# Seven products instead of eight in four more pairs of output blocks, with their sums gathered in one PSUM bank

## The chip, the cores and the metric

The kernel runs on one core of a Trainium2 chip. The metric is the device time of one execution in microseconds (us). In the text PE is TensorE (matmuls), ACT is ScalarE, DVE is VectorE, POOL is GpSimd and SP is SyncE, which here only issues transfers.

## The reference

Attention with a sliding window of 128 positions and a linear distance bias (8 batches of 8 heads, 576 positions, 64 channels) feeds a two-layer block with an ELU between the layers. All its 4608 rows go through both weight matrices:

```python
scores = scale * np.matmul(q, k.transpose(0, 1, 3, 2))        # 8 x 8 x 576 x 576
scores = np.where(mask, scores + bias[None], -1000000000.0)   # mask: 0 <= i - j < 128
attn = softmax(scores)
x = np.matmul(attn, v)  ->  (4608, 512)
h = x @ w_in                                                  # w_in 512 x 2048
g = np.where(h > 0.0, h, np.exp(np.minimum(h, 0.0)) - 1.0)
out = g @ w_out                                               # w_out 2048 x 512
```

## The kernel before, in words

The rows are taken in 9 tiles of 512. For each tile the *hidden* layer is made in 16 steps; in the later tiles a step is 256 rows by 2 chunks of 128 hidden channels: 8 matmuls of 256 columns (16 of 128 columns in earlier tiles) into one of two PSUM banks hp. ACT then takes an exponential into e, either by one step of ACT and a clamp on POOL (lines 310 and 311), or, where the step's slot is in the set SOFT, by two steps of ACT (307 and 308) and none of POOL. DVE combines e and the bank into g (`elu`, line 318), which also frees the bank for the hidden step after next.

Everything is laid out by hand in numbered *slots*. A slot holds one hidden step, the `elu` of the slot before, whatever stands in `tasks` for that slot (loads, transposes `turn_qk`, `weigh`, `all_values`, sums), a share of output in `OUT`, and what stands in `late` (combinations, attention `scores`). Each engine gets its instructions in the order in which the slots' lists are walked through, so what is queued ahead of what is decided here. Slot 24 has the hidden matmuls that start at 55.91 us of the profile, slot 42 those at 91.41, slot 88 those at 184.59, slot 134 those at 275.39 and slot 149, the last, those at 300.43.

The attention of a batch is four units of 128 keys. A unit puts its scores at the end of a slot; the next two slots each have two exponentials of ACT in front (`expo`, line 231) and one `weigh` on DVE (line 236); the slot after that has the product with v on PE (`all_values`), normalised by DVE and transposed into xT by a transfer from SP. This goes on until slot 133.

The *output* layer is made per pair n of two blocks of 128 rows (18 pairs). An ordinary pair takes 32 matmuls of 512 columns, 4 in each of 8 slots (`output`, line 324), a copy of each block by ACT (`store`, line 331) and a transfer from SP. The pairs in the list SEVEN, 11 of the 18, are computed as a 2 x 2 block product by seven multiplications (Winograd's form): g and w_out are cut in quarters, DVE makes four sums of g's quarters (`sums`, tiles S1 to S4, line 348, on 128 x 1024 elements in fp16), and once for all pairs four differences of w_out's quarters (`quarters`, tiles T1 to T4, in halves, in slots 25 to 32). Then seven products of 8 matmuls with 256 columns each follow (`product`, line 392), 7 matmuls in each of the pair's 8 slots, which begin at slot s = 15 + 8n. They are issued in the order of `turns`: 1, 6, 2, 7, 5, 4, 3.

The four output quarters are sums of the products: C11 = M1 + M2, U2 = M1 + M6, U3 = U2 + M7, C12 = U2 + M5 + M3, C22 = U3 + M5, C21 = U3 plus M4. Before the change ACT copies M1 out of PSUM into U1 and the finished C11 into the output tile ob, and DVE makes six additions per pair with one operand in PSUM (`combine`). Two banks (op and av, which change places after every such pair) each hold two halves:

```python
        turns = [(i, j) for i in (1, 6, 2, 7, 5, 4, 3) for j in range(8)]
        ...
        def places(n):
            x, y = XY[n]
            return ((x, 0), (y, 0), (x, 256), (y, 256)) if n < 2 * NTB - 1 else (
                (sp[2], 0), (sp[3], 0), (sp[0], 0), (hp[0], 0), (av, 0))
```

The last pair, 17, has no hidden steps beside it but the first ones, and is written out separately at the end of the slots (slots 148 to 152), with its last product split into two halves of 128 columns.

Of the kernel before, what the change touches and what calls it, by code (L numbers as in the profile page):

```python
# [18 lines left out]
def kernel(  # L19
# [9 lines left out]
    nc = tc.nc  # L29
    B, H, S, D = q.shape  # L30
    NTOK, DO = out.shape
    FF = moe_w_in.shape[1]
    NFC = FF // 128
    NTB = NTOK // 512
# [3 lines left out]
    V = nc.vector  # L38
# [35 lines left out]
    sp = [spa[:, 0, :], spa[:, 1, :]] + [ps_s.tile([128, 512], F32, name=f"sp{i}", tag=f"sp{i}") for i in (2, 3)]  # L74
    hp = [ps_h.tile([128, 512], F32, name=f"hp{i}", tag=f"hp{i}") for i in range(2)]
    av = ps_v.tile([128, 512], F32, name="av", tag="av")
# [72 lines left out]
    with tc.manual_schedule():  # L149
# [142 lines left out]
        def hidden(t, c0, w, f0, nf, p, soft):  # L292
            hps[t, c0, f0] = p
            a = (512 * t + c0) % RING
            cuts = [(0, w, a)] if a + w <= RING else [(0, RING - a, a), (RING - a, w, 0)]
            for l in range(nf):
                fc = f0 + l
                for u0, u1, x0 in cuts:
                    for c in range(4):
                        nc.tensor.matmul(  # L300
                            p[:, l * w + u0:l * w + u1], w_in_sb[:, c, fc * 128:(fc + 1) * 128],
                            xT[:, c, x0:x0 + u1 - u0], start=(c == 0), stop=(c == 3))
            e = es[t, c0, f0] = work.tile([128, 512], F32, name="e", tag="e", bufs=6)
            n = w * nf
            if soft:

                nc.scalar.activation(e[:, 0:n], p[:, 0:n], AF.Relu, scale=-1.0)  # L307
                nc.scalar.activation(e[:, 0:n], e[:, 0:n], AF.Exp, scale=-1.0)  # L308
                return
            nc.scalar.activation(e[:, 0:n], p[:, 0:n], AF.Exp)  # L310
            nc.gpsimd.tensor_scalar(out=e[:, 0:n], in0=e[:, 0:n], scalar1=1.0, scalar2=0.0,  # L311
                                    op0=ALU.min, op1=ALU.max)
# [25 lines left out]

        WB = lambda i, k: w_out_sb[:, 8 * i:8 * i + 8, 256 * k:256 * k + 256]

        def A(n, i, k):
            c = 256 * (n % 2) + 128 * i
            return gs[n // 2][:, 8 * k:8 * k + 8, c:c + 128]

        def add(o, a, b, op=ALU.add):
            V.tensor_tensor(out=o, in0=a, in1=b, op=op)  # L348

        def quarters(i, half):  # L350
            h = slice(4 * half, 4 * half + 4)
            a, b = {1: (WB(0, 1), WB(0, 0)), 2: (WB(1, 1), T[1]), 3: (WB(1, 1), WB(0, 1)), 4: (WB(1, 0), T[2])}[i]
            add(T[i][:, h, :], a[:, h, :], b[:, h, :], ALU.subtract)
# [8 lines left out]
                    3: lambda: (A(n, 0, 0), A(n, 1, 0)), 4: lambda: (A(n, 0, 1), SS[n, 2])}[i]()  # L362
            add(SS[n, i][:, j, :], a[:, j, :], b[:, j, :], ALU.add if i == 1 else ALU.subtract)

        def places(n):


            x, y = XY[n]
            return ((x, 0), (y, 0), (x, 256), (y, 256)) if n < 2 * NTB - 1 else (
                (sp[2], 0), (sp[3], 0), (sp[0], 0), (hp[0], 0), (av, 0))  # L370

        def place(n, i):
            o, c = places(n)[(0, 0, 4 if n == 2 * NTB - 1 else 2, 3, 2, 1, 1)[i - 1]]
            return o[:, c:c + 256]

        def kept(n, i):
            if (n, i) not in U:
                U[n, i] = work.tile([128, 256], F32, name=f"U{i}", tag=f"U{i}", bufs=1)
            return U[n, i]

        def tile_out(n, i):
            if (n, i) not in obs:
                obs[n, i] = work.tile([128, DO], F32, name="ob", tag="ob")
            return obs[n, i]

        def product(n, i, j0=0, j1=8, o=None, c0=0, c1=256):
            a, b = {1: lambda: (A(n, 0, 0), WB(0, 0)), 2: lambda: (A(n, 0, 1), WB(1, 0)), 3: lambda: (SS[n, 4], WB(1, 1)),
                    4: lambda: (A(n, 1, 1), T[4]), 5: lambda: (SS[n, 1], T[1]), 6: lambda: (SS[n, 2], T[2]),
                    7: lambda: (SS[n, 3], T[3])}[i]()
            o = place(n, i) if o is None else o  # L390
            for j in range(j0, j1):
                nc.tensor.matmul(o[:, 0:c1 - c0], a[:, j, :], b[:, j, c0:c1], start=j == 0 and (i in (1, 4, 5, 6) or o is av and n == 2 * NTB - 1),  # L392
                                 stop=j == 7, skip_group_check=True)
            if j1 == 8 and i == 1:
                nc.scalar.copy(kept(n, i), o)
            if j1 == 8 and i == 2:
                nc.scalar.copy(tile_out(n, 0)[:, 0:256], o)

        def combine(n, what):
            if what == "U2":  # L400
                add(kept(n, 2), kept(n, 1), place(n, 6))
            elif what == "U5":
                add(kept(n, 2), kept(n, 2), place(n, 5))
            elif what == "U3":
                add(kept(n, 3), kept(n, 1), place(n, 7))
            elif what == "C22":
                add(tile_out(n, 1)[:, 256:512], kept(n, 3), place(n, 5))
                if n == 2 * NTB - 1:
                    put(n, 1, 256, DO)
            elif what == "C12":  # L410
                add(tile_out(n, 0)[:, 256:512], kept(n, 2), place(n, 3))
                put(n, 0, 0, DO)
            else:
                add(tile_out(n, 1)[:, 0:256], kept(n, 3), place(n, 4))
                put(n, 1, 0, DO)

        def put(n, i, c0, c1):
            r = 256 * n + 128 * i
            nc.sync.dma_start(out[r:r + 128, c0:c1], tile_out(n, i)[:, c0:c1])

        def last_piece(n, o, c0, c1):
            product(n, 4, 0, 8, o, c0, c1)
            add(tile_out(n, 1)[:, c0:c1], kept(n, 3)[:, c0:c1], o[:, 0:c1 - c0])
            put(n, 1, c0, c1)

        wz = one([128, 256], F16, "wz")

# [69 lines left out]
        early, tasks, late, HID, OUT = {}, {}, {}, {}, {}  # L497

        def at(s, f, *a):
            tasks.setdefault(s, []).append((f, a))  # L500

        def after(s, f, *a):
            late.setdefault(s, []).append((f, a))

# [13 lines left out]
        for t in range(2, NTB):  # L518
            for j in range(16):
                step = (128 * (j // 4), 128, 4 * (j % 4), 4) if t < 4 else (256 * (j // 8), 256, 2 * (j % 8), 2)  # L520
                HID[16 * t + 6 + j] = [(t, *step, BUF[(j + 1) % 2])]
        SEVEN = (17, 3, 5, 7, 9, 11, 12, 13, 14, 15, 16)

        XY = {1: (op, av)}
        for n in range(2, 2 * NTB):
            XY[n] = XY[n - 1][::-1] if n - 1 in SEVEN else XY[n - 1]
        for o in range(16 * NTB):
            t, ts, f = o // 16, o // 4 % 4, o % 4
            if o // 8 in SEVEN:
                continue  # L530
            s = (9, 11, 13, 14)[o] if o < 4 else 11 + o if o < 13 else 2 * o - 1 if o < 16 else 15 + o
# [70 lines left out]
        for b in range(2, B):  # L602
            for u in range(4):
                a = START[b] + 4 * u
# [11 lines left out]
            a = START[b - 1] if b > 2 else 0  # L616
            for n in range(4):
                piece = (b, int(n < 2), n % 2)
                if b == 2:
                    m = 4 if n < 2 else 6  # L620
# [7 lines left out]
                at(a + 3 + n if a else 20 + n // 2, load_v, b, n)  # L628


        for m in range(8):
            at(25 + m, quarters, 1 + m // 2, m % 2)
        turns = [(i, j) for i in (1, 6, 2, 7, 5, 4, 3) for j in range(8)]
        for n in SEVEN:
            s = 15 + 8 * n
            if n < 2 * NTB - 1:
                m = 6 if n >= 8 else 4
                for d, i, j in ((-2, 1, (0, m)), (-1, 1, (m, 8)), (0, 2, ()), (1, 3, ()), (3, 4, ())):
                    at(s + d, sums, n, i, *j)
                for d, what in ((2, "U2"), (4, "U3"), (5, "C22"), (6, "C21"), (7, "C12")):  # L640
                    after(s + d, combine, n, what)
                for d in range(8):
                    OUT[s + d] = [(product, (n, i, j, j + 1)) for i, j in turns[7 * d:7 * d + 7]]
            else:
                at(s - 3, sums, n, 3)
                for i in (1, 2):
                    at(s - 2, sums, n, i, 0, 6)
                    at(s - 1, sums, n, i, 6, 8)
                at(s - 1, product, n, 1)
                at(s, sums, n, 4)  # L650
                OUT[s] = [(product, (n, 2)), (product, (n, 6)), (combine, (n, "U2")), (product, (n, 5)), (combine, (n, "U5"))]
                OUT[s + 1] = [(product, (n, 3)), (combine, (n, "C12")), (product, (n, 7)), (combine, (n, "U3"))]
                OUT[s + 2] = [(combine, (n, "C22")), (last_piece, (n, hp[0], 128, 256)), (last_piece, (n, hp[1], 0, 128))]


        SOFT = {s for n in SEVEN for s in range(13 + 8 * n, 19 + 8 * n)} | set(range(25, 33)) | set(range(16 * NTB - 10, 16 * NTB + 8))

        slots = set(HID) | set(OUT) | set(tasks) | set(early)
        for s in range(min(slots), max(slots) + 1):
            for f, a in early.get(s, []):  # L660
                f(*a)
            for step in HID.get(s, []):
                hidden(*step, s in SOFT)
            if s - 1 in HID and s not in (1, 4, 5):
# [37 lines left out]
```

## Time and profile before

| | us |
|---|---|
| median of 13 runs | 314.57 (314.21 to 316.31) |
| the profiled execution itself | 314.57 |
| its span, first to last instruction | 312.8 |
| PE busy | 304.8 |
| DVE busy | 247.4 |
| ACT busy | 215.8 |
| POOL busy | 124.1 |
| elu, DVE, 128x512 | 0.683 each, 144 of them |
| sums and quarters, DVE, 128x1024 fp16 | 0.66 to 0.68 each |
| additions, DVE, 128x256 with an operand in PSUM | 0.41 each |
| copies, ACT, 128x256 from PSUM | 0.353 each |
| copies, ACT, 128x512 from PSUM (store) | 0.58 each |

The difference of 1.8 us between the execution's time and its span lies around the first and the last instruction. The granted clock of PE is 1.0 throughout. Busy times of PE come from modelled ends and overlap, so that the distance between the starts of consecutive groups tells more than a single duration: a matmul of 256 columns has a duration of 273 ns but the next one starts about 110 ns later. On DVE and ACT too, the next instruction starts some 0.08 to 0.1 us before the row of the last one ends.

### The profile page before, as it was taken

The page shows a single profiled execution, that of the slowest core. Times are in us where ns is not written, and L with a number is a line of the kernel's source. Part 1 is how long each engine was busy: PE and PEld are TensorE (multiplying, and loading weights), DVE is VectorE, ACT ScalarE, POOL GpSimd, SP SyncE. Part 2 cuts the span into 40 slices and gives each one's busy share as a digit, 9 for nine tenths or more (in the row PEclk, how much of TensorE's full clock was granted, in tenths as well). Part 3 has the DMA queues.
Part 4 walks back from the last instruction along what each step waited for, and adds up shares of the span by engine and source line. Part 5 has one row for each costly group of instructions (what it writes and reads, how often), then busy time and mean ns, then how long its engine had stood idle before and what let it go on. Part 6 is the DMA issues. An engine that isn't in the chain of part 4 may idle for free.

```text
span 312.8 us, 10024 instructions
## 1 busy us (share of the span) xinstructions
PE 304.8 (97%) x4191; PEld 245.1 (78%) x4191; DVE 247.4 (79%) x489; ACT 215.8 (69%) x392; POOL 124.1 (40%) x190
## 2 busy tenths in 40 slices
PE   8899999999999999999999999999999999999995
PEld 6788874876788778987787678767889888888884
DVE  4747556898789878886897698778999889887883
ACT  4666458798686368656875588549787878768760
POOL 8947879611804562464336542663201010100000
PEclk9999999999999999999999999999999999999999
DMA  9999999990995939295929991999140202030102
GB/s 96 199 195 207 199 174 140 172 140 10 102 116 78 145 58 146 26 171 84 128 34 165 118 122 23 125 156 135 11 103 20 78 17 86 19 94 0 70 35 103
DMA packets 96510, 32.05 MB, mean 102 GB/s; under 512 B 83920, under 2 KB 91984, under 8 KB 96464
## 3 DMA queue, kind: packets, MB, share of 16 engines
q0 software_dynamic: 75920, 18.36, 64.3%
q1 hardware_dynamic: 20544, 13.05, 16.5%
q8 instruction: 33, 0.54, 0.8%
q14 instruction: 13, 0.11, 0.2%
HBM read 36.70 MB, written 9.44 MB: 148 GB/s over the span
## 4 chain that ended last, share of the span: by engine, by line
PE 79%; DVE 9%; DMA 4%; ACT 3%; issue 3%; POOL 1%; DVEq 0%; ACTq 0%; POOLq 0%
PE hp L300 34%; PE av L392 9%; PE op L392 8%; PE op L324 7%; PE av L324 5%; PE spa L225 4%; PE spa L266 3%; DVE g L318 2%; DMA st<-in_q_dram 2%; DMA VP<-in_v_dram 2%; PE op L430 2%; ACT EX L231 1%; DVE xn L255 1%; PE sp L300 1%; PE sp L392 1%
## 5 line engine op out<-in xcount | busy, mean ns | idle before, releaser
L300 PE MATMUL hp<-xT,wi 128*128 128x128 f16 (+2 forms) x1744 | 144.9, 233 | 2.0 <-DVE g L318 1.7
L300 PEld LDWEIGHTS <-wi 128*128 128x128 f16 x1856 | 124.5, 98 | 24.2 <-issue 7.5
L318 DVE SCALAR_TENSOR_TENSOR g<-e,hp 128x512 f16<-128x512 f32 x138 | 94.3, 683 | 25.1 <-POOL e L311 18.4
L311 POOL TENSOR_SCALAR e<-e 128x512 f32<-128x512 f32 x71 | 44.5, 627 | 146.7 <-ACT e L310 146.2
L310 ACT ACTIVATE e<-hp 128x512 f32<-128x512 f32 x65 | 38.9, 599 | 39.6 <-PE hp L300 36.3
L307 ACT ACTIVATE e<-hp 128x512 f32<-128x512 f32 x73 | 43.6, 598 | 21.2 <-PE hp L300 17.3
L308 ACT ACTIVATE e<-e 128x512 f32<-128x512 f32 x73 | 46.1, 631 | 2.3
L236 DVE TENSOR_TENSOR EX<-EX,TAB 128x1024 f16<-128x1024 f16 x48 | 33.2, 691 | 14.4 <-ACT EX L231 14.1
L392 PEld LDWEIGHTS <-S 128*128 128x128 f16 x352 | 32.9, 98 | 5.0 <-DVE S L348 1.4
L114 POOL DMA_DIRECT2D VP<-in_v_dram x40 | 34.4, 872 | 0.7 <-DVE xn L255 0.7
L324 PE MATMUL op<-wo,g 128*128 128x512 f16 x128 | 32.9, 379 | 0.0
L231 ACT ACTIVATE EX<-spa 128x512 f16<-128x512 f32 x48 | 26.0, 595 | 8.6 <-PE spa L225 7.5
L324 PEld LDWEIGHTS <-g 128*128 128x128 f16 x224 | 19.3, 97 | 14.8 <-issue 1.1
L392 PEld LDWEIGHTS <-g 128*128 128x128 f16 x272 | 25.2, 98 | 2.6
L231 ACT ACTIVATE EX<-sp 128x512 f16<-128x512 f32 x48 | 25.9, 595 | 0.0
L324 PE MATMUL av<-wo,g 128*128 128x512 f16 x80 | 20.5, 379 | 0.0
L392 PE MATMUL av<-s,S 128*128 128x256 f16 x120 | 18.0, 273 | 0.2 <-DVE S L348 0.2
L392 PE MATMUL op<-s,S 128*128 128x256 f16 x120 | 18.0, 273 | 0.1
L272 DVE TENSOR_TENSOR xn<-spa,rden 128x512 f16<-128x512 f32 x24 | 16.6, 692 | 0.8
L348 DVE TENSOR_TENSOR S<-g 128x1024 f16<-128x1024 f16 (+3 forms) x33 | 16.6, 502 | 0.2
L108 POOL DMA_DIRECT2D st<-in_k_dram x24 | 16.4, 686 | 0.4 <-issue 0.3
L108 POOL DMA_DIRECT2D st<-in_q_dram x24 | 16.2, 677 | 0.1
(142 smaller groups left out, 373.3 us busy)
## 6 DMA issues: line engine op xcount, KB each, us to landing
out_dram<-ob SPq DMA_DIRECT2D x35, 256.0 KB, 2.9
VP<-in_v_dram POOLq DMA_DIRECT2D x32, 128.0 KB, 5.0
st<-in_k_dram POOLq DMA_DIRECT2D x24, 144.0 KB, 4.2
st<-in_q_dram POOLq DMA_DIRECT2D x24, 144.0 KB, 4.6
wi<-in_moe_w_in_dram POOLq DMA_DIRECT2D x4, 512.0 KB, 11.0
wo<-in_moe_w_out_dram POOLq DMA_DIRECT2D x4, 512.0 KB, 10.3
VP<-in_v_dram POOLq DMA_DIRECT2D x8, 64.0 KB, 5.0
s<-in_k_dram POOLq DMA_DIRECT2D x1, 512.0 KB, 12.2
```

The costliest lines, as they stand in the source:

```text
L108: nc.gpsimd.dma_start(st[b][32 * g:32 * g + 32, w, :, :, :, :].rearrange("p h n j d -> p (h n) (j d)"), (q, k)[w][b, 2 * g:2 * g + 2, :, : ...
L114: nc.gpsimd.dma_start(VP[b % 2][0:p, n, :, 0:D], v[b, :, 128 * n:128 * n + p, :].rearrange("h p d -> p h d"))
L231: nc.scalar.activation(unit(b, u)[:, g, :, :], sp[g].rearrange("p (h c) -> p h c", h=2), AF.Exp, scale=0.125)
L236: V.tensor_tensor(out=e, in0=e, in1=TAB[:, int(u == 3), 2 * gp:2 * gp + 2, :, :], op=ALU.mult)
L300: nc.tensor.matmul(p[:, l * w + u0:l * w + u1], w_in_sb[:, c, fc * 128:(fc + 1) * 128], xT[:, c, x0:x0 + u1 - u0], start=(c == 0), stop=(c ...
L307: nc.scalar.activation(e[:, 0:n], p[:, 0:n], AF.Relu, scale=-1.0)
L308: nc.scalar.activation(e[:, 0:n], e[:, 0:n], AF.Exp, scale=-1.0)
L310: nc.scalar.activation(e[:, 0:n], p[:, 0:n], AF.Exp)
L311: nc.gpsimd.tensor_scalar(out=e[:, 0:n], in0=e[:, 0:n], scalar1=1.0, scalar2=0.0, op0=ALU.min, op1=ALU.max)
L318: V.scalar_tensor_tensor(out=gs[t][:, f0:f0 + nf, c0:c0 + w], in0=sh(es.pop((t, c0, f0))), scalar=1.0, in1=sh(hps.pop((t, c0, f0))), op0=A ...
L324: nc.tensor.matmul(o, gs[t][:, fc, ts * 128:(ts + 1) * 128], w_out_sb[:, fc, :], start=(fc == 0), stop=(fc == NFC - 1))
L392: nc.tensor.matmul(o[:, 0:c1 - c0], a[:, j, :], b[:, j, c0:c1], start=j == 0 and (i in (1, 4, 5, 6) or o is av and n == 2 * NTB - 1), stop ...
```

## The change

The pairs 3 to 17 are all taken by seven products (15 instead of 11; pairs 4, 6, 8 and 10 are new). The order of the products becomes 1, 2, 6, 5, 7, 3, 4. Products 1, 6, 7 and 4 now add up in one bank z, one after the other: after 1, 6 and 7 ACT copies the running sum (M1, U2, U3) out, and after 4 the bank holds C21, which ACT copies into the output tile. In the other bank x stand first product 2, then 5, which overwrites it, then 3, which is added onto 5; ACT copies M5 out before 3 is added. DVE is left with three additions per pair: C11 = U1 + x, C12 = U6 + x, and C22 = U7 + U5, whose operands both lie in SBUF. So each pair has five copies of ACT and three additions of DVE, where it had two and six.

The sums of DVE move to the front of their slots (`at_once`, behind the elu of the slot before), S1 is made in one piece, and the halves of w_out's differences move to slots 26, 30, 31, 32, 34, 35, 36 and 39. SOFT, the slots in which ACT takes both steps of the hidden layer, follows the sums. For the last pair the fourth product is made in one piece, and its two halves are copied by ACT and by DVE and sent from ACT's and SP's queues.

```diff
         def place(n, i):
-            o, c = places(n)[(0, 0, 4 if n == 2 * NTB - 1 else 2, 3, 2, 1, 1)[i - 1]]
-            return o[:, c:c + 256]
+            z, x = XY[n] if n < 2 * NTB - 1 else (sp[2], sp[3] if i == 2 else sp[0])
+            return (z if i in (1, 4, 6, 7) else x)[:, 0:256]
...
-                nc.tensor.matmul(o[:, 0:c1 - c0], a[:, j, :], b[:, j, c0:c1], start=j == 0 and (i in (1, 4, 5, 6) or o is av and n == 2 * NTB - 1),
-                                 stop=j == 7, skip_group_check=True)
-            if j1 == 8 and i == 1:
+                nc.tensor.matmul(o, a[:, j, :], b[:, j, :], start=j == 0 and i in (1, 2, 5), stop=j == 7,
+                                 skip_group_check=True)
+            if j1 == 8 and i in (1, 5, 6, 7):
                 nc.scalar.copy(kept(n, i), o)
-            if j1 == 8 and i == 2:
-                nc.scalar.copy(tile_out(n, 0)[:, 0:256], o)
+            if j1 == 8 and i == 4 and n < 2 * NTB - 1:
+                nc.scalar.copy(tile_out(n, 1)[:, 0:256], o)
...
         def combine(n, what):
-            if what == "U2":
-                add(kept(n, 2), kept(n, 1), place(n, 6))
-            elif what == "U5":
-                add(kept(n, 2), kept(n, 2), place(n, 5))
-            elif what == "U3":
-                add(kept(n, 3), kept(n, 1), place(n, 7))
...
+            if what == "C11":
+                add(tile_out(n, 0)[:, 0:256], kept(n, 1), place(n, 2))
             elif what == "C12":
-                add(tile_out(n, 0)[:, 256:512], kept(n, 2), place(n, 3))
+                add(tile_out(n, 0)[:, 256:512], kept(n, 6), place(n, 3))
                 put(n, 0, 0, DO)
             else:
-                add(tile_out(n, 1)[:, 0:256], kept(n, 3), place(n, 4))
-                put(n, 1, 0, DO)
...
+                add(tile_out(n, 1)[:, 256:512], kept(n, 7), kept(n, 5))
+                put(n, 1, 0 if n < 2 * NTB - 1 else 256, DO)
...
+        def last_out(n):
+            o = place(n, 4)
+            for c0, copy, queue in ((0, nc.scalar.copy, nc.scalar), (128, V.tensor_copy, nc.sync)):
+                copy(tile_out(n, 1)[:, c0:c0 + 128], o[:, c0:c0 + 128])
+                put(n, 1, c0, c0 + 128, queue)
...
+        def at_once(s, f, *a):
+            tasks.setdefault(s, []).insert(0, (f, a))
...
-        SEVEN = (17, 3, 5, 7, 9, 11, 12, 13, 14, 15, 16)
+        SEVEN = range(3, 18)
...
-        for m in range(8):
-            at(25 + m, quarters, 1 + m // 2, m % 2)
-        turns = [(i, j) for i in (1, 6, 2, 7, 5, 4, 3) for j in range(8)]
+        for m, a in enumerate((26, 30, 31, 32, 34, 35, 36, 39)):
+            at_once(a, quarters, 1 + m // 2, m % 2)
+        turns = [(i, j) for i in (1, 2, 6, 5, 7, 3, 4) for j in range(8)]
...
-                m = 6 if n >= 8 else 4
-                for d, i, j in ((-2, 1, (0, m)), (-1, 1, (m, 8)), (0, 2, ()), (1, 3, ()), (3, 4, ())):
-                    at(s + d, sums, n, i, *j)
-                for d, what in ((2, "U2"), (4, "U3"), (5, "C22"), (6, "C21"), (7, "C12")):
-                    after(s + d, combine, n, what)
+                for d, i in ((-1, 1), (1, 2), (3, 3), (4, 4)):
+                    at_once(s + d, sums, n, i)
+                after(s + 2, combine, n, "C11")
+                after(s + 6, combine, n, "C12")
+                at_once(s + 8, combine, n, "C22")
...
-                OUT[s] = [(product, (n, 2)), (product, (n, 6)), (combine, (n, "U2")), (product, (n, 5)), (combine, (n, "U5"))]
-                OUT[s + 1] = [(product, (n, 3)), (combine, (n, "C12")), (product, (n, 7)), (combine, (n, "U3"))]
-                OUT[s + 2] = [(combine, (n, "C22")), (last_piece, (n, hp[0], 128, 256)), (last_piece, (n, hp[1], 0, 128))]
+                OUT[s] = [(product, (n, 2)), (combine, (n, "C11")), (sums, (n, 4)), (product, (n, 6)), (product, (n, 5))]
+                OUT[s + 1] = [(product, (n, 7)), (product, (n, 3)), (combine, (n, "C12")), (combine, (n, "C22")),
+                              (product, (n, 4)), (last_out, (n,))]
...
-        SOFT = {s for n in SEVEN for s in range(13 + 8 * n, 19 + 8 * n)} | set(range(25, 33)) | set(range(16 * NTB - 10, 16 * NTB + 8))
+        SOFT = {15 + 8 * n + d for n in SEVEN for d in (0, 1, 2, 3, 4, 7)} | {26, 30, 31, 32, 34, 35, 36, 39} | set(range(16 * NTB - 10, 16 * NTB + 8))
```

## The prediction

> **What bounds the kernel now.** I read the busy shares first, then the chain that ended last, then that chain in order of time at three places, and last the timelines of TensorE (PE) and ScalarE (ACT) side by side.
>
> ```profile
> PE 304.8 (97%) x4191; PEld 245.1 (78%) x4191; DVE 247.4 (79%) x489; ACT 215.8 (69%) x392; POOL 124.1 (40%) x190
> PE 79%; DVE 9%; DMA 4%; ACT 3%; issue 3%; POOL 1%; DVEq 0%; ACTq 0%; POOLq 0%
> ```
>
> A busy PE isn't always PE at its rate, so the chain counts for more: 79% of it is PE, and in order of time it shows whether one group follows the other without a hole. First an ordinary pair, then a pair by seven products:
>
> ```profile
> 201.32 0.86 PE op L324 x4
> 202.18 0.87 PE hp L300 x8
> 203.05 0.86 PE op L324 x4
> 203.92 0.87 PE hp L300 x8
> ...
> 289.13 0.87 PE hp L300 x8
> 290.00 0.77 PE op L392 x7
> 290.77 0.87 PE hp L300 x8
> ```
>
> The starts differ by exactly the durations. A slot (one hidden step and its share of output) costs 0.87 + 0.86 = 1.73 us in an ordinary pair and 0.87 + 0.77 = 1.64 us in a seven-product pair, plus the attention that lies in it (about 0.65 for scores, 0.5 for values). PE's own work is the bound from 70 us on, but for small holes. The largest cluster lies where VectorE (DVE) forms the differences of w_out's quarters, rows "s":
>
> ```profile
> 66.04 0.57 DVE s L348
> 66.61 0.29 DVE g L318
> 66.90 0.23 issue
> 67.13 0.68 DVE EX L216
> 67.81 0.60 DVE s L348
> 68.41 0.61 DVE g L318
> 69.02 0.04 issue
> 69.06 1.05 PE hp L300 x16
> ```
>
> DVE is the chain from 59.7 to 69.0 us, and a hidden step starts when DVE's elu (g L318) has freed its bank. The holes that I find by taking each slot's groups off the distance between hidden starts: 0.24 + 0.37 + 0.43 = 1.04 us before the steps at 61.50, 67.26 and 69.06; 0.59 before 95.78; and 0.30, 0.33, 0.20, 0.26, 0.26, 0.48 before 122.16, 218.60, 234.33, 257.59, 273.27 and 277.51, 1.83 together. So 3.5 us of PE idling behind DVE or ACT is all there is besides PE's work.
>
> How far ACT runs behind PE, in the stretch without attention (PE's last matmul of product 1, then ACT):
>
> ```profile
> 280.02 0.27 PE L392 MATMUL op<-wo,g 128*128 128x256 f16 x1
> ...
> 280.85 0.63 ACT L308 ACTIVATE e<-e 128x512 f32<-128x512 f32 x1
> 281.38 0.35 ACT L395 COPY U<-op 128x256 f32<-128x256 f32 x1
> ```
>
> The product is complete at 280.29 and its copy at 281.73, 1.44 us later, because ACT's two steps of the hidden slot stand ahead of it.
>
> **The change, part by part.** The profiled execution took 314.57 us (span 312.8 and 1.8 around it), which is the median; the sum is made against it. About 0.2% (0.6 us) is what a measurement of this kernel can tell from no change.
>
> *Four more pairs by seven products (4, 6, 8, 10).* Each changes 32 matmuls of 512 columns into 56 of 256. By rows: 8 slots x (1.73 - 1.64), or 32 x 0.216 - 56 x 0.1095 = 6.91 - 6.13 = 0.78 us a pair, all on the bound: **-3.1 us**. Here a rule of the Trainium skill speaks against the change: "TensorE: Matmul & The Clock Gate", section "Back-to-back issue gap", gives a sustained spacing of some 81 ns at 128 columns and 131 ns at 512, since loads and matmuls are pipelined together. An estimate from it, with 98 ns for 256 on the line between, makes an ordinary pair 32 x 131 = 4.2 us and seven products 56 x 98 = 5.5 us, so +5.2 us for four pairs. The rows say 0.86/4 = 215 ns at 512 columns and 0.77/7 = 110 at 256: cost goes with columns, and the 12.5% fewer columns are nearly all kept. I take the rows.
>
> *w_out's quarters.* The eight 1024-column differences (0.68 us, 0.60 from start to start) stay eight, but stand in slots 26, 30, 31, 32, 34, 35, 36, 39 instead of 25 to 32. By slot 29 DVE has one of them behind it, not five, so 4 x 0.6 = 2.4 us less stands before the elu that PE waits for: 1.04 us of holes goes, and I count **-1.0** (between 0 and -1.0). What is late next: slots 34 to 40, where they now lie. Adding DVE's rows per slot gives 10.6 us for slots 34 to 39 against 11.7 of PE, so it is covered, without much to spare. Slots 25, 27, 28, 29 go from ACT's second step (0.63) to POOL's (0.63) behind POOL's load issues (0.68 each); PE's 1.45 to 1.98 a slot cover both. The quarters issue no DMA; they pass the turn_qk transposes of slots 32 to 37 on DVE, nothing on SP or POOL.
>
> *DVE per seven-product pair.* Before: four sums (2.4 us start to start) and six adds from PSUM (0.33 each, row 0.41). After: four sums and three adds, so 1.0 us less a pair. The third, C22, reads two SBUF tiles; no row shows that for 256 fp32 columns, and I take the PSUM form's 0.41 (between 0.28 and 0.42, worth 0.1 us a pair either way, covered). The four new pairs add 3.4 us of DVE each. From slot 40 to 104 DVE then needs 112 us against PE's 122 (before 102 of 125): nearer to PE, never above it. The sums now follow the elu at once. DVE waits 14.1 us in total for ACT's exponentials in front of its weighing (EX L236), and a sum fills that wait instead of queueing behind it: at 93.17 DVE waits 0.28, then weighs, transposes and sums, and the ready elu comes at 95.05, with PE idle 0.41 behind it. Of the 2.42 us of other holes I count half: **-1.2** (between 0 and -2.4).
>
> *ACT.* The copies 128x256 go from 22 to 74 (0.353 us, 0.25 start to start), stores 128x512 from 14 to 6 (0.58), and 21 more hidden steps take the second step on ACT (0.63): +18.4 - 4.6 + 13.3 = +27 us, 243 us of some 309, 79%. All beside PE while ACT keeps up. The new wait is the point of danger: products 1, 6, 7, 4 share one bank, so product 6 may not start before ACT has copied 1, nor 7 before 6, nor 4 before 7; and 3 adds onto 5. Between the end of a product and the start of the next one in its bank PE has the eight matmuls of another product and one hidden step: 8 x 0.11 + 0.87 = 1.75 us for ACT to copy. The rows above took 1.44. Behind a waiting product stand the rest of PE's slot and the next hidden step, hence ACT's next steps, so a late copy delays but doesn't pile up. Where two slots with exponentials and copies follow each other ACT needs 2 x 0.49 + 1.16 + 0.25 = 2.39 us against PE's 1.65, twice, and then 0.75 of 2.15. Before had 2.39 + 2.14 in slots 88 and 89, and PE's starts stand 1.65, 1.64, 2.27 us apart: 0.15 lost. Going along slots 50 to 53 by hand, with these durations, each copy lands 0.05 to 0.3 us ahead of need. Bounds: 0, and 0.1 on each of 56 hand-overs, 5.6. I take the row near it: 7 such places at 0.15, **+1.0**. C11 must be read before product 5 overwrites its bank, 1.75 us as well; DVE has two rows ahead of it there, covered.
>
> *End.* Before, the last product ends at 309.13 and the adds of its two halves at 309.55. After, product 4 ends at the same place and is copied in two halves; in the built program VectorE's copy waits for ScalarE's, since both read one bank: two times about 0.28 (row 128x128, 280 ns) gives 309.75. **+0.2** (between -0.2, if C22's move clears DVE earlier, and +0.5). One store of 64 KB moves from SP to ACT's queue, last on both; of the others SP issues 37 instead of 38 and waits behind the same transposes.
>
> Sum: -3.1 - 1.0 - 1.2 + 1.0 + 0.2 = -4.1, so **310.5 us**. The parts' bounds reach from 308 to 317.
>
> **The rivals.** *A: half of it is lost.* DVE stays as late as it was (its stretch 40 to 56 fills 29.0 of 30.3 us, the densest of all) and ACT's hand-overs cost 1.5: -3.1 - 0.5 + 1.5 + 0.2 = -1.9, **312.7 us**. For it: in the two densest DVE slots of before (42 and 133, 2.5 us in 1.65 and 2.13) PE did wait, and slot 46 now becomes a third. Against: these waits came with six adds and late sums.
>
> *B: ACT's hand-over becomes the bound; slower.* The other parts are worth -5.1, so it decides from 5.1/56 = 0.09 us a hand-over on. If the copies behind exponentials come 0.2 late in half of the 56 and the reactions on ACT's next steps make that 6.3 in sum, the time is **315.8 us**. For it: margin of 0.31 without attention, less 0.25 if another copy stands ahead. Against: slots 88 and 89, and the slots with scores or values, where PE takes 0.5 to 0.65 longer and ACT catches up.
>
> *C: better than counted.* DVE's holes all go and ACT costs nothing: -3.1 - 1.0 - 2.4 + 0.2, **308.3 us**.
>
> **Chances.** The forecast's case 0.57, A 0.23, B 0.10, C 0.07, something that makes no difference (the pairs' gain just eaten) 0.03. The range leaves out most of B and C: 308.9 to 313.8. A's upper tail reaches "no change", so faster 0.86, same 0.05, slower 0.09.
>
> **What would show it.** Right: 96 matmuls 128x512 of L324 instead of 224 and 840 products; 1.64 us slots in the pairs 4, 6, 8, 10; no DVE chain between 59 and 69 us; waits of PE's products on ACT's U below 1.5 us in total; ACT near 243 us busy. Wrong: rows "PE op/av <- ACT U" of several us, slots of 1.8 us and more in seven-product pairs (B), or the chain with DVE's g L318 in front of hidden steps between 95 and 130 us (A). If the slots of the new pairs stay at 1.73, the first step is false.

## The result and the profile after

The changed kernel takes **311.67 us** (median of 11 runs, 311.22 to 312.36) against 314.77 for the kernel before on the same chips (48 runs). The ratio is **0.9894, with a 95% interval of 0.9878 to 0.9911**: faster by 3.1 us by the medians and 3.3 by the ratio, where the forecast said 4.1 and rival A 1.9. The profiled execution took 311.22 us, of which the span is 309.4; the 1.8 us around the span are as before. The profiled executions of e1, e2 and e3 below, and only these, start slot 24 some 2 us later than the others (58.05, 57.68 and 57.89 us against 55.6 to 56.2), so the experiments compare what comes from slot 24 on.

First the page of the changed kernel: the busy times of the engines, and the shares of the chain that ended last.

```profile
PE 301.9 (98%) x4279; PEld 254.3 (82%) x4279; DVE 251.4 (81%) x484; ACT 238.0 (77%) x458; POOL 111.3 (36%) x169
PE 69%; DVE 9%; issue 7%; ACT 6%; POOL 4%; DMA 3%; POOLq 0%; DVEq 0%; ACTq 0%
...
L388 PEld LDWEIGHTS <-S 128*128 128x128 f16 x480 | 45.2, 98 | 4.9
L388 PEld LDWEIGHTS <-g 128*128 128x128 f16 x360 | 33.7, 98 | 3.5
```

The weight loads of line 388 count the products: 480 + 360 = 840, eight for each of 105. ACT stands at 238 us; 243 was expected. PE's share of the chain has gone down from 79% to 69%: the other engines stand in the chain more often.

A pair that is newly taken by seven products (pair 8), in the chain in order of time:

```profile
167.00 0.87 PE hp L300 x8
167.87 0.11 PE av L388
167.98 0.66 PE op L388 x6
168.63 0.87 PE hp L300 x8
```

From hidden step to hidden step (167.00 to 168.63) the new pair takes 1.63 us, like the old ones in the prediction's lines (1.64). Four products in one bank do not disturb this slot: its pieces in `av` and `op` follow each other without a gap.

The ledger below is read from the starts of the hidden steps (L300) in PE's timeline of both kernels, slot by slot. Slot 24 starts at 55.91 before and 55.70 after, and nothing of the change lies ahead of it, so 0.21 of the difference is the start's own scatter. From slot 24 to slot 149 the kernel before takes 244.52 us and the changed one 241.46, **-3.06**. From the last slot's start to the end of the span it is 12.36 and 12.28.

| where | predicted | measured |
|---|---|---|
| four pairs, without the stalls listed below | -3.1 | -2.9 (pairs 4, 6, 8, 10: -0.81, -0.66, -0.71, -0.69) |
| slots 24 to 31, w_out's quarters | -1.0 | -0.35 |
| holes that closed: slots 43, 56, 104, 112, 124, 132, 134 | -1.2 for both rows | -1.8 |
| holes behind DVE that opened: slots 39, 47, 103, 111 | | +1.0 |
| slots 52, 69, 77, 120, 128, ACT late | +1.0 | +1.4 |
| other slots (60 and 72 above all) | 0 | -0.4 |
| behind the last hidden step | +0.2 | -0.1 |
| ahead of slot 24 | 0 | -0.2 |

In slots 47, 52 and 69, which lie in new pairs, the stall is counted from the length that a seven-product slot should have, 2.13, 1.91 and 1.91 us.

### The profile page after: what moved, and what is told of

It reads as the page before. It is cut to its first block, busy times and chain, and to the rows that moved or that the text cites. A ratio compares the mean times of both kernels' runs of the same rounds, so it can differ in the third digit from the quotient of the medians.

```text
span 309.4 us, 10228 instructions
## 1 busy us (share of the span) xinstructions
PE 301.9 (98%) x4279; PEld 254.3 (82%) x4279; DVE 251.4 (81%) x484; ACT 238.0 (77%) x458; POOL 111.3 (36%) x169
## 4 chain that ended last, share of the span: by engine, by line
PE 69%; DVE 9%; issue 7%; ACT 6%; POOL 4%; DMA 3%; POOLq 0%; DVEq 0%; ACTq 0%
PE hp L300 30%; PE op L388 11%; PE av L388 11%; DVE g L318 3%; PE spa L225 3%; PE op L324 3%; DMA wi<-in_moe_w_in_dram 3%; ACT EX L231 2%; PE spa L266 2%; POOL e L311 2%; ACT e L310 2%; PE sp L388 1%; DVE EX L236 1%; PE sp L324 1%; PE sp L300 1%
## 5 line engine op out<-in xcount | busy, mean ns | idle before, releaser
L300 PE MATMUL hp<-xT,wi 128*128 128x128 f16 (+2 forms) x1744 | 144.9, 233 | 1.3 <-DVE g L318 0.5
L300 PEld LDWEIGHTS <-wi 128*128 128x128 f16 x1856 | 124.4, 98 | 19.1 <-issue 6.4
L318 DVE SCALAR_TENSOR_TENSOR g<-e,hp 128x512 f16<-128x512 f32 x138 | 93.7, 679 | 25.8 <-ACT e L308 12.6
L311 POOL TENSOR_SCALAR e<-e 128x512 f32<-128x512 f32 x50 | 31.3, 627 | 159.1 <-ACT e L310 158.7
L307 ACT ACTIVATE e<-hp 128x512 f32<-128x512 f32 x94 | 56.2, 598 | 25.4 <-PE hp L300 21.9
L308 ACT ACTIVATE e<-e 128x512 f32<-128x512 f32 x94 | 59.3, 631 | 3.0
L388 PEld LDWEIGHTS <-S 128*128 128x128 f16 x480 | 45.2, 98 | 4.9
L236 DVE TENSOR_TENSOR EX<-EX,TAB 128x1024 f16<-128x1024 f16 x48 | 33.4, 695 | 6.0 <-ACT EX L231 5.8
L388 PEld LDWEIGHTS <-g 128*128 128x128 f16 x360 | 33.7, 98 | 3.5
L388 PE MATMUL op<-s,S 128*128 128x256 f16 x168 | 25.2, 272 | 0.0
L388 PE MATMUL av<-s,S 128*128 128x256 f16 x168 | 25.2, 272 | 0.0
L349 DVE TENSOR_TENSOR S<-g 128x1024 f16<-128x1024 f16 (+2 forms) x31 | 20.8, 670 | 0.8 <-PE av L388 0.2
L388 PE MATMUL av<-wo,g 128*128 128x256 f16 x112 | 16.8, 272 | 0.0
L388 PE MATMUL op<-wo,g 128*128 128x256 f16 x112 | 16.8, 272 | 0.0
L324 PE MATMUL op<-wo,g 128*128 128x512 f16 x64 | 16.4, 379 | 0.0
```

The lines of the kernel that those rows point to most:

```text
L236: V.tensor_tensor(out=e, in0=e, in1=TAB[:, int(u == 3), 2 * gp:2 * gp + 2, :, :], op=ALU.mult)
L300: nc.tensor.matmul(p[:, l * w + u0:l * w + u1], w_in_sb[:, c, fc * 128:(fc + 1) * 128], xT[:, c, x0:x0 + u1 - u0], start=(c == 0), stop=(c ...
L318: V.scalar_tensor_tensor(out=gs[t][:, f0:f0 + nf, c0:c0 + w], in0=sh(es.pop((t, c0, f0))), scalar=1.0, in1=sh(hps.pop((t, c0, f0))), op0=A ...
L324: nc.tensor.matmul(o, gs[t][:, fc, ts * 128:(ts + 1) * 128], w_out_sb[:, fc, :], start=(fc == 0), stop=(fc == NFC - 1))
L388: nc.tensor.matmul(o, a[:, j, :], b[:, j, :], start=j == 0 and i in (1, 2, 5), stop=j == 7, skip_group_check=True)
```

## The experiments

The last column is the time from the start of slot 24's hidden step to that of slot 149, in the one profiled execution of each kernel. Most slots that a change does not touch agree to 0.02 us from kernel to kernel; the times of whole executions scatter by far more.

| kernel | time, us (runs) | ratio to before, 95% interval | slot 24 to 149, us |
|---|---|---|---|
| before | 314.77 (48) | | 244.52 |
| after | 311.67 (11) | 0.9894, 0.9878 to 0.9911 | 241.46 |
| e1_pairs_only | 312.71 (9) | 0.9938, 0.991 to 0.9966 | 242.39 |
| e2_scheme_eleven | 314.13 (12) | 0.9964, 0.994 to 0.9988 | 243.19 |
| e3_sums_behind | 312.75 (9) | 0.9935, 0.9913 to 0.9958 | 242.36 |
| e4_copies_twice | 321.39 (6) | 1.0196, 1.0167 to 1.0225 | 250.95 |
| e5_quarters_s1_behind | 310.56 (6) | 0.987, 0.9846 to 0.9894 | 240.28 |
| e6_quarters_behind | 310.90 (1) | | 241.25 |
| e7_copy5_later | 311.89 (5) | 0.9906, 0.9889 to 0.9924 | 241.75 |
| e8_soft38 | 310.95 (1) | | 241.27 |
| e9_soft_68_76 | 310.98 (5) | 0.9847, 0.9821 to 0.9873 | 240.13 |

### Four more pairs, in the scheme of before (e1)

```diff
 (kernel before)
-        SEVEN = (17, 3, 5, 7, 9, 11, 12, 13, 14, 15, 16)
+        SEVEN = range(3, 18)
```

> The kernel before with the four pairs 4, 6, 8, 10 added to SEVEN and nothing else changed (old order of products, six additions by VectorE). Theory: PE's saving of 3.1 us is real in any form, but VectorE's six additions and late sums can't be paid in consecutive pairs (119 us of VectorE against 122 of PE in slots 40 to 104), so about 3 us of it comes back as elu waits: 314.0 (313.0 to 315.5), and hidden steps wait for VectorE in the new pairs. Rival: the gain comes from the four pairs alone and the rest of the change is idle: 311.6.

Measured: 312.71 us, below the range of the theory. From slot 24 to 149 it gains 2.13 of the 3.1 us that the seven products can bring, so the old scheme, with six additions of DVE per pair, loses a third of it and not most. By the slots: pair 6 gains 0.76 and pair 8 0.75, which is the predicted 0.78 nearly in full; pair 10 gains 0.61; pair 4 loses 0.22. There the chain of this kernel in order of time shows what it costs to have the additions and S1 ahead of the elu:

```profile
104.22 0.77 DVE QT L145
104.99 0.31 DVE S L348
105.30 0.33 DVE ob L348
105.63 0.61 DVE g L318
106.23 0.04 issue
106.28 0.77 PE hp L300 x11
```

A transpose, a part of a sum and an addition follow each other, the elu (g L318) comes behind all of them, and PE's hidden step 0.65 us after the elu's start. Slot 47 takes 2.71 us where 2.13 would do.

### The new scheme for the old eleven pairs (e2)

```diff
 (kernel after)
-        SEVEN = range(3, 18)
+        SEVEN = (3, 5, 7, 9, 11, 12, 13, 14, 15, 16, 17)
```

> The changed kernel with the old eleven pairs only (4, 6, 8, 10 ordinary again). Theory: keeps the holes that the change closed in slots 43, 56, 104, 112, 134 (about 1.9 us) and the 0.35 around the quarters, loses the pairs' saving of about 2 net: 313.3 (312.6 to 314.0). Rival that the new sums and copies bring nothing by themselves: 314.7, as before.

Measured: 314.13 us, -1.33 from slot 24 to 149. The scheme alone brings -1.33 and the pairs alone -2.13, which makes -3.46; both together bring -3.06. So the two parts nearly add up, with 0.4 us lost where both act at once, and the new scheme is not what makes the new pairs pay: the pairs bring 2.1 us in the old scheme and 1.7 in the new one.

### VectorE's sums and quarters behind the rest of their slots (e3)

```diff
 (kernel after)
-            at_once(a, quarters, 1 + m // 2, m % 2)
+            at(a, quarters, 1 + m // 2, m % 2)
...
-                    at_once(s + d, sums, n, i)
+                    at(s + d, sums, n, i)
...
-                at_once(s + 8, combine, n, "C22")
+                at(s + 8, combine, n, "C22")
```

> The changed kernel with sums, C22 and the quarters' halves at the end of their slots' lists instead of in front (slots and all else as changed). Theory: the front position fills VectorE's waits for exponentials, so its loss costs 1 to 1.5 us of elu waits: 312.8 (312.2 to 313.5). Rival: the front position takes as much from the weighing and the values (slots 27, 31, 103, 111, 120, 128 lost 1.0 us) as it brings: 311.7, within 0.4.

Measured: 312.75 us. From slot 24 to 149 it is 0.90 slower than the changed kernel. But the difference has two signs. At slot 40 this kernel is 0.65 us ahead of the changed one; after that it loses 1.55 on balance. Slots 43, 49, 57, 91, 100, 121 and 129 lose 0.15 to 0.37 each; 47, 93, 103 and 111 gain 0.12 to 0.28. So the place in front is wrong for the quarters, and right for some of the sums and wrong for others. This led to e5. Of the seven holes that the change closed, only slot 43 opens again in full (2.71 us) and 124 and 132 by half: 1.36 of the 1.84 us stays gone though the sums stand behind.

### Every kept copy twice (e4)

```diff
 (kernel after)
             if j1 == 8 and i in (1, 5, 6, 7):
                 nc.scalar.copy(kept(n, i), o)
+                nc.scalar.copy(kept(n, i), o)
```

> The changed kernel with each of the 60 copies of products 1, 5, 6, 7 by ScalarE made twice, so that each hand-over of a bank comes 0.25 us later and ScalarE has 15 us more to do. Theory (the hand-overs have slack, lateness acts through e and the elu): 2 to 4 us more than the changed kernel, 314.5 (313.3 to 316), with no rows of a product waiting for U. Rival (the hand-over itself is at its limit, as in case B of the prediction): 0.15 or more on each of 56, above 319, with such rows. A third possibility, ScalarE far from any limit: under 312.3.

Measured: 321.39 us, far above what the theory gave; the rival, that the hand-over has no room left, is right. Here is the tightest of a pair's hand-overs in the changed kernel, in a stretch without attention, first PE's timeline and then ACT's (start, duration, instruction):

```profile
276.75 0.27 PE L388 MATMUL op<-wo,g 128*128 128x256 f16 x1
276.86 0.82 PE L388 MATMUL av<-wo,g 128*128 128x256 f16 x6
277.51 1.04 PE L300 MATMUL hp<-xT,wi 128*128 128x256 f16 x8
278.38 0.38 PE L388 MATMUL av<-wo,g 128*128 128x256 f16 x2
278.60 0.71 PE L388 MATMUL op<-s,S 128*128 128x256 f16 x5
```

```profile
277.57 0.63 ACT L308 ACTIVATE e<-e 128x512 f32<-128x512 f32 x1
278.11 0.35 ACT L391 COPY U<-op 128x256 f32<-128x256 f32 x1
```

Product 1 ends in op at 277.02, its copy at 278.46, and product 6 enters op at 278.60: **0.14 us to spare**. With the second copy, at the same place (slot 137; PE, then ACT):

```profile
287.09 0.38 PE L388 MATMUL av<-wo,g 128*128 128x256 f16 x2
287.63 0.70 PE L388 MATMUL op<-s,S 128*128 128x256 f16 x5 [0.15 <-DVE g L318]
```

```profile
286.82 0.35 ACT L391 COPY U<-op 128x256 f32<-128x256 f32 x1
287.20 0.37 ACT L392 COPY U<-op 128x256 f32<-128x256 f32 x1
```

The copies end at 287.57 and product 6 starts at 287.63, where 287.31 would follow from its predecessor (287.09 and two pieces of 0.11). The slot takes 1.95 us instead of 1.64. No product in op or av starts sooner than 0.05 us behind the copy that it needs here, so of the 0.14 only some 0.09 could be used up. With attention it is closer still: in slots 52, 73 and 81 of the changed kernel the next product starts 0.06 to 0.07 us behind the copy, while the other three hand-overs of the pair above leave 0.31 to 0.58. The releaser that the profile names in brackets, an elu of DVE, had long been done; the copy is what came last. Five waits of other products are put down to ACT's U in this profile, 1.0 us in sum. So the change stands just on the near side of rival B: 0.38 us more per copy and 60 copies make +9.5 us between slots 24 and 149, and the kernel is slower than before.

### The quarters and S1 behind, S2 to S4 in front (e5), and the quarters alone (e6)

```diff
 (kernel after)
-            at_once(a, quarters, 1 + m // 2, m % 2)
+            at(a, quarters, 1 + m // 2, m % 2)
...
-                    at_once(s + d, sums, n, i)
+                    (at if i == 1 else at_once)(s + d, sums, n, i)
```

> The changed kernel with the halves of w_out's differences and the sums S1 behind the other VectorE work of their slots, S2, S3, S4 and C22 still in front. Theory (a sum in front is right where VectorE would wait for exponentials, and wrong where it delays values or weighing that PE takes in the next slot): slots 27, 31 and 39 lose their waits of 0.22, 0.16 and 0.28, slots 103 and 111 those of 0.27 and 0.12, and nothing comes back: 1.0 us less than the changed kernel, 310.7 (310.2 to 311.2). Rival: what is late is ScalarE and the order on VectorE only moves the wait: 311.7.

> The changed kernel with the quarters' halves alone behind. Theory: slots 27 and 31 take 1.97 and 2.28 instead of 2.20 and 2.44, slot 39 keeps 2.4 (there S1 of slot 38 in front of the weighing is to blame, not a quarter); 0.4 us less. Rival for slot 39: the quarter there is to blame, then 2.14.

Measured: e5 310.56 us, the fastest so far, though its interval overlaps that of the changed kernel; e6, with only the first of the two edits, 310.90 in one run. From slot 24 to 149 e5 takes 1.18 us less than the changed kernel. The slots say where: 27 (2.20 to 1.98), 31 (2.44 to 2.28), 39 (2.42 to 2.14), 47 (2.44 to 2.32), 103 (2.17 to 1.90) and 111 (2.26 to 2.14). Only slot 28 gives 0.05 back. In e6 slots 27 and 31 shorten alike, and 39 keeps its 2.41, so it is S1 and not a quarter that slot 39 pays for. DVE's timeline of slot 27 in the changed kernel, then in e5:

```profile
60.35 0.69 DVE L318 SCALAR_TENSOR_TENSOR g<-e,hp 128x512 f16<-128x512 f32 x1 [0.29 <-POOL e L311]
60.96 0.69 DVE L349 TENSOR_TENSOR s<-wo 128x1024 f16<-128x1024 f16 x1
61.56 0.18 DVE L254 RECIPROCAL rden<-av 128x4 f32<-128x4 f32 x1
61.77 0.42 DVE L255 TENSOR_TENSOR xn<-av,rden 128x256 f16<-128x256 f32 x1
```

```profile
60.65 0.69 DVE L318 SCALAR_TENSOR_TENSOR g<-e,hp 128x512 f16<-128x512 f32 x1 [0.29 <-POOL e L311]
61.25 0.18 DVE L254 RECIPROCAL rden<-av 128x4 f32<-128x4 f32 x1
61.46 0.42 DVE L255 TENSOR_TENSOR xn<-av,rden 128x256 f16<-128x256 f32 x1
61.80 0.68 DVE L349 TENSOR_TENSOR s<-wo 128x1024 f16<-128x1024 f16 x1
```

Normalised values (xn) feed transposes on PE in the same slot (L284), so a quarter ahead of them goes straight into PE's time. The chain of the changed kernel goes through this place: quarter, xn until 62.20, and the transposes at 62.25.

### The copy of product 5 behind the exponentials (e7)

```diff
 (kernel e5)
-            if j1 == 8 and i in (1, 5, 6, 7):
+            if j1 == 8 and i in (1, 5, 6, 7) and (n, i) not in LATER:
...
+        LATER = ((6, 5), (7, 5))
+
+        def copy_out(n, i):
+            nc.scalar.copy(kept(n, i), place(n, i))
...
+                if (n, 5) in LATER:
+                    at_once(s + 5, copy_out, n, 5)
```

> As e5, and ScalarE's copy of product 5 for pairs 6 and 7 moves behind the next slot's exponentials and hidden step (slots 68 and 76). Theory (ScalarE in two adjacent slots with exponentials is what makes elu late in slots 69 and 77): 0.25 us less in each, 0.5 less than e5: 310.2. Rival: product 3 then waits for the copy, no gain or 0.3 more than e5.

Measured: 311.89 us, slower than e5. The rival is right. Product 3, which is added onto product 5 in the same bank, begins at the end of slot s + 5, not in the next one, so the later copy stops PE itself:

```profile
143.16 0.71 PE L388 MATMUL av<-s,S 128*128 128x256 f16 x5
144.78 0.38 PE L388 MATMUL op<-wo,S 128*128 128x256 f16 x2 [0.91 <-ACT U L398]
```

Slots 68 and 76 take 2.73 and 2.82 us instead of 1.66 and 1.64; slots 69 and 77 come back to 1.91 and 2.12. The lateness moved by one slot and grew. Since everything behind the stopped product was late too, the short slots 69 and 77 are no proof that this copy was their cause.

### Slot 38 with both steps on ACT (e8)

```diff
 (kernel after)
-        SOFT = {...} | {26, 30, 31, 32, 34, 35, 36, 39} | ...
+        SOFT = {...} | {26, 30, 31, 32, 34, 35, 36, 38, 39} | ...
```

> The changed kernel with ScalarE instead of GpSimd taking the clamp of the hidden step in slot 38. Theory (the weighing of slot 38, 1.10 us instead of 0.69, is slowed by GpSimd's clamp that runs beside it, both reading two or one operands of SBUF): the weighing takes 0.69 and slot 39 2.14 instead of 2.42. Rival (order alone): slot 39 stays at 2.4.

In the changed kernel slot 38 is no longer in SOFT, so POOL clamps there, and S1 in front moves the weighing (EX L236) on DVE to the same time. DVE, then POOL:

```profile
84.31 0.69 DVE L349 TENSOR_TENSOR S<-g 128x1024 f16<-128x1024 f16 x1
84.91 1.10 DVE L236 TENSOR_TENSOR EX<-EX,TAB 128x1024 f16<-128x1024 f16 x1
85.93 0.67 DVE L318 SCALAR_TENSOR_TENSOR g<-e,hp 128x512 f16<-128x512 f32 x1
```

```profile
84.71 0.76 POOL L311 TENSOR_SCALAR e<-e 128x512 f32<-128x512 f32 x1 [0.30 <-ACT e L310]
```

Without POOL's clamp, in e8:

```profile
84.83 0.68 DVE L236 TENSOR_TENSOR EX<-EX,TAB 128x1024 f16<-128x1024 f16 x1
85.43 0.68 DVE L318 SCALAR_TENSOR_TENSOR g<-e,hp 128x512 f16<-128x512 f32 x1
```

Measured: 310.95 us in one run; the weighing takes 0.68 instead of 1.10, and slot 39 2.14 instead of 2.42; slot 47 takes 0.08 more, and from slot 24 to 149 it is 0.19 less than the changed kernel. So the two engines do hold each other up: the clamp takes 0.76 too, where 0.61 is usual. PE feels it in slot 39, where the product with v loads its weights from the weighed tile:

```profile
86.06 0.30 PEld L266 LDWEIGHTS <-EX 128*128 128x128 f16 x8 [0.22 <-DVE EX L236]
```

The Trainium skill, "SBUF — State Buffer", section "Who interferes with whom", says of the ports that DVE and GpSimd share that they are "an exclusive lock". The rows agree, and another meeting in the changed kernel shows how it goes. DVE's weighing of slot 29 and the elu behind it, then POOL's clamp:

```profile
66.41 0.68 DVE L216 TENSOR_TENSOR EX<-EX,TAB 128x1024 f16<-128x1024 f16 x1
67.60 0.69 DVE L318 SCALAR_TENSOR_TENSOR g<-e,hp 128x512 f16<-128x512 f32 x1 [0.51 <-POOL e L311]
```

```profile
66.72 0.84 POOL L311 TENSOR_SCALAR e<-e 128x512 f32<-128x512 f32 x1 [0.32 <-ACT e L310]
```

The weighing began first and keeps its usual time; the clamp takes 0.84 and ends 0.47 us behind it. In slot 38 the clamp ends 0.47 behind S1, too (85.47 and 85.00), and the weighing, third in the row, 0.54 behind the clamp. So the operation that comes second waits, and the first one loses nothing. In e5 the weighing stands ahead of the clamp and keeps its 0.68, and S1 behind it takes 1.10 in its place; PE does not wait for S1 there, and slot 39 takes the same 2.14.

### Slots 68 and 76 with both steps on ACT (e9)

```diff
 (kernel e5)
-        SOFT = {...} | {26, 30, 31, 32, 34, 35, 36, 39} | ...
+        SOFT = {...} | {26, 30, 31, 32, 34, 35, 36, 39, 68, 76} | ...
```

> The kernel is e5_quarters_s1_behind (310.56 us, slots 69 and 77 of 2.37 and 2.47 us against 2.01 and 2.12 in the kernel before) with the slots 68 and 76 in SOFT: ACT takes both steps of the hidden layer there instead of one step and POOL's clamp. In the profile of e5 DVE waits 0.57 us in slot 69 for POOL's clamp, which began 0.29 after ACT's exponential and took 0.61. Theory (the hand-over from ACT to POOL and POOL's own time are what is late): ACT's second step follows its first after 0.53 and takes 0.63, so e is ready about 0.2 to 0.3 us earlier; slots 69 and 77 shorten by 0.2 each, and the time is 310.1 us. Rival (ACT itself is late, not POOL): the copy of a product that now stands behind the second step comes 0.53 us later and a product waits for it, the next exponential too; slots 69 and 77 stay or grow by 0.1 to 0.3, and the time is 310.6 to 311.1 us.

Measured: 310.98 us, ratio 0.9847; the interval overlaps that of e5, so by the times the two are the same. By the slots, 69 takes 2.26 instead of 2.37 and 77 2.32 instead of 2.47: the theory's direction, at little more than half of its size. The wait that was on POOL for 0.57 us is now on ACT for 0.46:

```profile
145.60 0.69 DVE L318 SCALAR_TENSOR_TENSOR g<-e,hp 128x512 f16<-128x512 f32 x1 [0.46 <-ACT e L308]
```

Taking POOL out was worth 0.1 to 0.15 us a slot, and the wait that is left is for ACT. From slot 24 to 149 it takes 240.13 us against e5's 240.28. I did not try to spread ACT's exponentials otherwise.

## Why the prediction was right, and where its sum was off

**Four pairs, -3.1.** Right: -2.9 without the stalls. The rule of spacing that I weighed against the rows (131 and 81 ns a matmul) would have made these pairs 5.2 us longer; pairs 6 and 8 in e1 gain 0.76 and 0.75 us each. The rows decide.

**The quarters, -1.0.** The mis-sized term; -0.35. The reason given was right as far as it went: with fewer differences ahead of it, the elu of slots 26, 29 and 30 comes earlier (slot 29: 2.18 to 1.81), and these slots lose 0.72 of the 1.04 us. What the step missed is that I had asked only what stands ahead of the elu. `at_once` puts the quarter ahead of the slot's own tasks, and in slots 27 and 31 PE waits for one of these, xn, within the slot. By e6 that is 0.37 us of the missing 0.65. Nearly all the rest, 0.27, is in slot 30, where the elu waits 0.51 us for POOL's clamp of slot 29 (the rows at 67.60 and 66.72 in e8). Before, ACT took both steps there; the prediction gave this slot to POOL with 0.63 us for the clamp, called it covered, and did not ask what DVE does beside it. Beside the weighing it takes 0.84. No run put this slot back on ACT. That DVE had time enough over slots 34 to 39 (10.6 of 11.7 us) held: slots 32 to 38 are unchanged to 0.01 us.

**DVE's order and fewer additions, -1.2.** The closed holes are 1.8 us, more than the half that I counted, but 1.0 came new, so the sum is -0.85. The reason was in part another: DVE's waits for exponentials ahead of its weighing did go down from 14.1 to 5.8 us, but by e3 only 0.5 us of the closed holes needs the sums in front. The rest comes with fewer additions, the other order of products and the new SOFT together; no run takes these apart. "A sum fills that wait instead of queueing behind it" is true only where the sum is shorter than the wait: in slot 102 of before DVE waits 0.28 between elu and weighing, and of after S1 stands there, 0.60 from start to start. The weighing starts 1.34 us behind the elu instead of 0.97, the product with v that reads it comes later in slot 103, and e5, with S1 behind, has slot 103 back at 1.90. Of the new holes I had named one (slot 46 into 47); slot 39 is DVE beside POOL, by e8.

**ACT, +1.0.** The size is too small (+1.4), and the way is another. I had looked for it in products that wait for a copy. No product waits for ACT's U in the changed kernel. The loss is in five slots behind two slots with exponentials each, where ACT itself is the chain and DVE's elu waits:

```profile
109.95 0.34 PE hp L300 x7
110.29 0.99 ACT EX L231 x2
111.27 0.50 ACT e L307
...
111.79 0.64 ACT e L308
...
112.45 0.70 DVE g L318
...
113.19 0.83 PE hp L300 x12
```

PE's step at 113.19 is released by a chain that goes back through elu, two steps and two exponentials to a step of 109.95. In slots 120 and 128 the elu waits for ACT just as long, and they keep their 2.22 us whether the sums stand in front (changed kernel) or behind (e3), so DVE's order is not the cause there:

```profile
246.21 0.69 DVE L318 SCALAR_TENSOR_TENSOR g<-e,hp 128x512 f16<-128x512 f32 x1 [0.46 <-ACT e L308]
```

In slots 69 and 77 POOL's clamp stands between ACT and the elu as well, and e9 puts its share at 0.1 to 0.15. ACT now has 52 more copies and 21 more second steps, and in front of these exponentials stands one of the copies (109.94 in ACT's timeline); which of the two makes it late I have not separated, and e7 does not tell. The walk by hand over slots 50 to 53 (0.05 to 0.3 us ahead of need) was right for the copies (0.06 in slot 52) and did not follow the elu that ACT's next steps release: slot 52 is one of the five.

**The room of the hand-over, 0.31.** Mis-sized: it is 0.14, and 0.06 to 0.07 in the three closest slots. The window that I wrote, 8 x 0.11 + 0.87 = 1.75, is counted from the start of one piece to the next; from the product's end, at 277.02, to product 6 at 278.60 it is 1.58, since the last matmul of 0.27 us still runs for 0.17 after its successor has started. ACT's 1.44 was as before. Rival B was therefore nearer than its 0.10, as e4 shows: nothing else was needed but a longer copy.

**The end, +0.2.** The step itself held and was the wrong place to stop. Product 4 ends 8.69 us behind the last hidden step's start (8.70 before), and its two half copies follow each other:

```profile
304.96 0.89 PE sp L388 x8
...
305.88 0.27 ACT ob L412
...
306.17 0.29 DVE ob L412
```

The last copy ends 0.61 us behind the product, instead of 0.42: +0.19. But the span ends with the transfers, and it is 0.08 shorter from the last hidden step on. SP's last issues, two before and one after, and the one that moved to ACT's queue:

```profile
309.60 0.89 SPq L419 DMA_DIRECT2D out_dram<-ob  x2
```

```profile
306.49 0.34 SPq L407 DMA_DIRECT2D out_dram<-ob  x1
306.17 0.38 ACTq L407 DMA_DIRECT2D out_dram<-ob  x1
```

Before, the two halves were stored by SP one after the other, and the second issue was done 1.36 us behind the product's end. Now one half goes by ACT's queue, SP issues the other as soon as its copy ends (306.46), and is done 0.98 us behind the product: 0.38 sooner, in spite of the later copies. Most of it is lost again in the last transfer, which lands 1.51 us behind the end of its issue instead of 1.20. The prediction named the move of a store to ACT's queue and gave it no price.

The sum came to -4.1; the spans of the two profiled executions differ by 3.35. It has 0.65 too much for the quarters, 0.35 for DVE's order, 0.2 for the pairs and 0.4 too little loss for ACT, 1.6 together. Against these stand 0.85 of gain that it did not have: other slots, the end, and the start, where the last is scatter. That the sum came as near as it did is therefore partly luck. The signs are mixed in the same way. The 96 matmuls of L324, the 840 products, the slots of 1.63 us and the absence of waits for U came as named. But a quarter still stands in the chain at 61 us, and a sign of rival A came too: in the chain between 95 and 130 us the elu stands in front of a hidden step in slots 47 and 52.

## What to carry to other kernels

Moving an operation to the front of an engine's list must be weighed against every consumer behind it in that stretch, the one in the same slot too, and not only against the one that the move is meant to serve: here S2 to S4 belonged in front, S1 and the quarters behind, and the mixed order takes 1.2 us less than the changed kernel from slot 24 to 149, in one profile of each (310.56 us as a whole; the intervals of the ratios overlap). A hand-over window is counted from the producer's end to the consumer's start, and doubling the suspected work is a cheap way to learn how much room is left. Where an engine becomes fuller, look for the price in what it feeds last in the stretch, not only in the instruction that was added.

## What the runs showed of the hardware that was not expected

DVE's weighing of 128x1024 took 1.10 us instead of 0.69 behind a clamp of POOL, and 0.68 without it; a clamp behind a weighing took 0.84 instead of 0.61, and the weighing its usual 0.68. The second one pays.

A product that adds onto a bank started 0.05 us behind the end of ACT's copy of it at the earliest (e4), with 0.35 us for the copy.

PE's granted clock can fall after a short idle stretch. In e1's profile PE waits 1.38 us for a load of q that lands at 8.57 us; from 10 to 12 us its clock stands at 0.50, and at 1.00 again from 13 us on. In e2 and e3 PE waits 1.11 and 1.62 us for the same load, and the clock falls to 0.50 likewise. In the other eight profiles the longest wait for it is 0.33 us, and the clock stays at 1.00. So of e1's 2.1 us up to slot 24 the late load takes about half, by PE's start of that work (8.61 instead of 7.48); the rest is lost in the slower stretch behind it. That the wait sets off the drop was not tried by an experiment.
